# Expert stage of a delta-rule and routing kernel: 31 tiles of 128 tokens in place of 19 tiles of 256

## The chip, the cores and the metric

The kernel runs on one core of one Trainium2 chip. The metric is device time in microseconds (us), the median of several executions. One execution was also recorded by the hardware profiler, instruction by instruction. The engines are named as in its rows: PE (TensorE matmuls), PEld (TensorE weight loads, which overlap PE), DVE (VectorE), ACT (ScalarE), POOL (GpSimd) and SP (SyncE, which here only issues transfers). A "q" behind a name, as in SPq, is that engine's sequencer.

## The reference

Four sequences of 768 tokens, 8 heads of 48, go through a delta rule, and each of the 3072 output rows of 384 then goes through one of 8 experts. Everything is float32.

```
for t in range(S):                       # per batch and head
    y[t]  = q[t] @ state
    state = state + beta[t] * outer(k_n[t], v[t] - k_n[t] @ state)
x = y as [3072, 384]
expert_idx = argmax(cosine(x, expert_emb) / tau);  gate = softmax(...)[expert_idx]
for e in range(8):                       # w1[e]: 384 x 1024, w2[e]: 1024 x 384
    mask = expert_idx == e
    out[mask] = gate[mask] * (relu(x[mask] @ w1[e]) @ w2[e])
```

## The kernel before

The delta rule is worked in chunks of 128 tokens, six chunks of each sequence; a chunk inverts a 128 x 128 triangular matrix per head in six levels (`invert`: transposes on L240, products on L248 and L257, all 128 x 128). The chunk's rows and their gates are stored to `x_dram`, and each token's number is scattered into `idmap`, a list per expert in DRAM (L362, four scatters a chunk, on POOL's queue).

When all tokens are routed, a few short VectorE operations (L400 to L421) work out, for each of the tiles that the experts then run, which expert it has and where its part of the list begins. The number of tiles is fixed in the program: N / T + E - 1 with N = 3072 and E = 8, which is 19 for T = 256. It is enough for any split of the tokens; tiles that the split does not need run all the same, on list entries that name a row of zeros, and their output rows are dropped.

For a tile, `fetch(i)` reads expert and place into registers of SP and issues on SP's queue, in this order, the tile's list `ids`, the expert's `w1` (384 x 1024, 1536 KB) and its `w2` (1024 x 384, 1536 KB). POOL gathers the tile's rows `xg` from `x_dram` by those `ids`, 128 rows to an instruction. `experts` transposes the rows on PE (L447), copies them to `xTm` on DVE (L448), multiplies `w1` into `psH` (L454, moving operand 256 columns wide), applies Relu on ACT (L456), multiplies by `w2` for each half of 128 tokens (L460, moving operand 384 wide), scales by the gate on DVE (L463) and scatters the rows to `out` from POOL (L464). The pool `wt` holds the weights in two buffers, so a load of `w1` waits until PE is done with the `w1` of two tiles before.

A float32 matmul stands as two instructions in the trace (24 matmuls of L454 in a tile are 48 records), a transpose as one. The order on each engine comes from the framework's scheduler, which lets it differ a little from the order in the code.

Of the kernel before, what the change touches and what calls it, by code (L numbers as in the profile page):

```python
# [8 lines left out]
F32 = mybir.dt.float32  # L9
I32 = mybir.dt.int32  # L10
AX = mybir.AxisListType
ALU = mybir.AluOpType
ACT = mybir.ActivationFunctionType
SP = mybir.EngineType.SP

C = 128  # tokens in a chunk of the delta rule
T = 256  # tokens in a tile of the experts
LEVELS = (2, 4, 8, 16, 32, 64)
# [3 lines left out]
def kernel(  # L22
# [11 lines left out]
):  # L34
    """Delta rule in chunks of 128 tokens, then each token through its one expert, all in float32.

    In a chunk, with kb = beta k and the state S before it, z solves (I + A) z = v - k S, with
    A[t, s] = k_t . kb_s below the diagonal; then y = q S + strict_lower(q kb^T) z and S += kb^T z.
    (I + A)^-1 is put together from its diagonal blocks, of 2, 4, ... 128 rows: from the inverses of
    blocks of s rows to those of 2s rows, W = W - W A_s^T W, where W is the transposed inverse and  # L40
    A_s the part of A below the diagonal blocks of s inside those of 2s.

    A token's rank within its expert gives its place in a list of that expert's tokens (in DRAM).
    The experts then work through tiles of 256 tokens of one expert each; 256-token tiles that any
    split of the tokens needs are at most N / 256 + E - 1, and those it doesn't need are empty.
    """
    nc = tc.nc
    B, H, S, D = q.shape
    NC, NP, Dm, N = S // C, H // 2, H * D, B * S
    E, _, F = moe_w1.shape  # L50
    KC, NF = Dm // 128, F // 128
    NT = N // T + E - 1
# [4 lines left out]
    x_dram = tc.dram_tile([N + 1, Dm + 1], F32, name="x_dram")  # L57
    idmap = tc.dram_tile([NMAP, 1], I32, name="idmap")

    def big(shape):  # L60
        return ps.tile(shape, F32, name="big", tag="big", bufs=5)

    def seq(shape):
        return ps.tile(shape, F32, name="seq", tag="seq", bufs=3)

# [1 line left out]
    ident = cpool.tile([128, 128], F32, name="ident")  # L67
    make_identity(nc, ident)
    ones = cpool.tile([128, 128], F32, name="ones")
# [17 lines left out]

    # Tokens' lists name the row of zeros behind the tokens wherever no token is put in.
    none = cpool.tile([128, NMAP // 128], I32, name="none")
# [13 lines left out]

    # With x = row ^ column, x in [s, 2s) picks the blocks of s rows beside the diagonal ones.
    xor_i = ac.tile([128, 128], I32, name="xor_i")
# [23 lines left out]

# [1 line left out]
    Qp = []  # L131
    for i in range(2):
        t = ac.tile([128, B, H, 64], F32, name=f"Qp{i}")
# [3 lines left out]
    for i in range(6):  # L137
        t = ac.tile([128, 2, H, 64], F32, name=f"KK{i}")
# [27 lines left out]

    # Expert embeddings over their norms, transposed.
    esq = ac.tile([E, Dm], F32, name="esq")
# [11 lines left out]

# [1 line left out]
    def prep(c, K4):  # L182
        """k over its norm, and that times beta, padded to 64 columns a head."""
        Ksq = wk.tile([128, B, H, D], F32, name="Ksq", tag="Ksq", bufs=1)
        nc.gpsimd.tensor_tensor(Ksq, K4, K4, op=ALU.mult)
        rn = wk.tile([128, B, H], F32, name="rn", tag="rn")
        nc.vector.tensor_reduce(rn, Ksq, axis=AX.X, op=ALU.add)
        nc.gpsimd.tensor_tensor(out=rn, in0=rn, in1=half, op=ALU.pow)
        nc.vector.tensor_scalar_add(rn, rn, 1e-6)
        nc.vector.reciprocal(rn, rn)  # L190
        kks = []
        for b in range(B):
            kk = KK[(c * B + b) % len(KK)]
            nc.gpsimd.tensor_tensor(kk[:, 0, :, 0:D], K4[:, b],
                                    rn[:, b].unsqueeze(2).broadcast_to([128, H, D]), op=ALU.mult)
            nc.gpsimd.tensor_tensor(kk[:, 1, :, 0:D], kk[:, 0, :, 0:D],  # L196
                                    betaT[:, c, b].unsqueeze(2).broadcast_to([128, H, D]), op=ALU.mult)
            kks.append(kk)
        return kks

    def front(c, b, kk):
        """Transposes of k, q and kb, and the two masked products over kb."""
        KT = wk.tile([128, NP, 3, 128], F32, name="KT", tag="KT", bufs=3)
# [29 lines left out]
    def invert(groups):  # L233
        """groups: [A^T by head, W], W the transposed inverses of the diagonal blocks of 2 rows."""
        for s in LEVELS:
# [17 lines left out]
            for g, Pm in zip(groups, Ps):  # L253
                W = g[1]
# [8 lines left out]
    def back(c, b, kk, KT, LM, Ws, V, xc, ssx, lz):  # L263
        """The chunk's outputs and the next state; the logits and the norms of the outputs."""
        if c > 0:
# [39 lines left out]
        psX = big([128, KC, 128])  # L305
# [9 lines left out]
    def route(c, xc, ssx, lz):  # L315
        """Each token's expert, gate and place in its expert's list, for a chunk of each sequence."""
        def t(name, shape):
# [9 lines left out]
        nc.vector.tensor_reduce(m, lz, axis=AX.X, op=ALU.max)  # L327
        # The first of the largest.
        oh = t("oh", be)
# [56 lines left out]

# [1 line left out]
    wt = ctx.enter_context(tc.tile_pool(name="wt", bufs=2))  # L388
    mk = ctx.enter_context(tc.tile_pool(name="mk", bufs=2))
# [32 lines left out]

# [1 line left out]
    def fetch(i):  # L424
        e = nc.values_load(info[0:1, 0, i:i + 1], engines=(SP,), min_val=0, max_val=E - 1)
        s = nc.values_load(info[0:1, 1, i:i + 1], engines=(SP,), min_val=0, max_val=NMAP - T)
        ids = mk.tile([128, 2], I32, name="ids", tag="ids", bufs=4)
        nc.sync.dma_start(ids, idmap[bass.ds(s, T), :].rearrange("(p t) o -> p (t o)", t=2))
        w1 = wt.tile([128, KC, F], F32, name="w1", tag="w1")
        nc.sync.dma_start(w1, moe_w1[bass.ds(e, 1)].rearrange("o (c p) f -> p (o c) f", p=128))  # L430
        w2 = wt.tile([128, NF, Dm], F32, name="w2", tag="w2")
        nc.sync.dma_start(w2, moe_w2[bass.ds(e, 1)].rearrange("o (f p) m -> p (o f) m", p=128))
        xg = []
        for t in range(2):
            x = mk.tile([128, Dm + 1], F32, name="xg", tag="xg", bufs=6)
            nc.gpsimd.indirect_dma_start(  # L436
                out=x, out_offset=None, in_=x_dram[:, :],
                in_offset=bass.IndirectOffsetOnAxis(ap=ids[:, t:t + 1], axis=0))
            xg.append(x)
        return ids, w1, w2, xg  # L440

    def experts(ids, w1, w2, xg):
        xT = mk.tile([128, KC, T], F32, name="xTm", tag="xTm")
        for t in range(2):
            psX = big([128, KC, 128])
            for j in range(KC):
                nc.tensor.transpose(psX[:, j, :], xg[t][:, j * 128:(j + 1) * 128], ident)  # L447
            nc.vector.tensor_copy(xT[:, :, t * 128:(t + 1) * 128], psX)  # L448
        hT = mk.tile([128, NF, T], F32, name="hT", tag="hT")
        for f in range(0, NF, 2):  # L450
            psH = big([128, 2, T])
            for i in range(2):
                for j in range(KC):
                    nc.tensor.matmul(psH[:, i, :], lhsT=w1[:, j, (f + i) * 128:(f + i + 1) * 128], rhs=xT[:, j, :],  # L454
                                     start=(j == 0), stop=(j == KC - 1))
            nc.scalar.activation(hT[:, f:f + 2, :], psH, ACT.Relu)  # L456
        for t in range(2):
            psO = seq([128, Dm])
            for f in range(NF):
                nc.tensor.matmul(psO, lhsT=hT[:, f, t * 128:(t + 1) * 128], rhs=w2[:, f, :],  # L460
                                 start=(f == 0), stop=(f == NF - 1))
            y = mk.tile([128, Dm], F32, name="y", tag="y", bufs=4)
            nc.vector.tensor_scalar_mul(y, psO, xg[t][:, Dm:Dm + 1])  # L463
            nc.gpsimd.indirect_dma_start(  # L464
                out=out[:, :], out_offset=bass.IndirectOffsetOnAxis(ap=ids[:, t:t + 1], axis=0),
                in_=y, in_offset=None, bounds_check=N - 1, oob_is_err=False)

    ahead = fetch(0)
    for i in range(NT):
        now = ahead  # L470
        if i + 1 < NT:
            ahead = fetch(i + 1)
        experts(*now)

# [29 lines left out]
```

## Time and profile before

| | |
|---|---|
| time, three executions | 1692.67, 1698.79, 1700.02 us |
| median | 1698.79 us |
| span of the profiled execution, first to last instruction | 1703.2 us |
| PE busy over the span | 1476.8 us (87%) |
| mean granted clock of TensorE | 0.864 |
| first L454 matmul starts, last L463 starts | 1262.20 us, 1692.24 us |

No other time was recorded for the profiled execution than its span, which lies 4.4 us above the median. Busy times are sums over records, and a record's own duration overlaps its neighbours' where an engine is pipelined, as PE is: the pace of matmuls is read from when one line's records start to when the next line's start. [...]

### The profile page before, as it was taken

The page shows a single profiled execution, that of the slowest core. Times are in us where ns is not written, and L with a number is a line of the kernel's source. Part 1 is how long each engine was busy: PE and PEld are TensorE (multiplying, and loading weights), DVE is VectorE, ACT ScalarE, POOL GpSimd, SP SyncE. Part 2 cuts the span into 40 slices and gives each one's busy share as a digit, 9 for nine tenths or more (in the row PEclk, how much of TensorE's full clock was granted, in tenths as well). Part 3 has the DMA queues.
Part 4 walks back from the last instruction along what each step waited for, and adds up shares of the span by engine and source line. Part 5 has one row for each costly group of instructions (what it writes and reads, how often), then busy time and mean ns, then how long its engine had stood idle before and what let it go on. Part 6 is the DMA issues. An engine that isn't in the chain of part 4 may idle for free. (4 is left out here: it accounts for less than half of the span.)

```text
span 1703.2 us, 23067 instructions
## 1 busy us (share of the span) xinstructions
PE 1476.8 (87%) x9723; PEld 1318.2 (77%) x9723; DVE 568.2 (33%) x1015; ACT 318.2 (19%) x613; POOL 350.3 (21%) x330
## 2 busy tenths in 40 slices
PE   3698969989698997989889897989739999999997
PEld 2697959979597996979789796979737666677774
DVE  4542525344362543526343352625401111001010
ACT  2122222121222212122212212222100000111110
POOL 7703042020503004030310204020021111111110
PEclk9786959789697977969788896979769999999999
DMA  9100030001200010000100000000045554555540
GB/s 144 19 1 10 1 65 1 6 5 20 47 1 10 1 43 6 1 10 1 38 1 1 1 1 19 2 1 1 19 171 184 173 180 159 163 179 178 165 145 0
DMA packets 114233, 92.62 MB, mean 54 GB/s; under 512 B 81137, under 2 KB 103849, under 8 KB 114130
## 3 DMA queue, kind: packets, MB, share of 16 engines
q1 hardware_dynamic: 108290, 78.80, 16.3%
q0 software_dynamic: 5632, 12.24, 2.6%
q8 instruction: 76, 1.25, 0.3%
q14 instruction: 27, 0.22, 0.0%
q10 hardware_dynamic: 208, 0.11, 0.0%
HBM read 81.55 MB, written 12.33 MB: 55 GB/s over the span
## 5 line engine op out<-in xcount | busy, mean ns | idle before, releaser
L251 DVE TENSOR_TENSOR Pm<-big,nmask 128x512 f32<-128x512 f32 x288 | 198.1, 691 | 308.8 <-PE big L248 308.8
L248 PE MATMUL big<-Ti,LM 128*128 128x128 f32 x2304 | 290.7, 288 | 0.0
L248 PEld LDWEIGHTS big<-Ti,LM 128*128 128x128 f32 x2304 | 285.9, 206 | 0.0
L257 PE MATMUL big<-W,Pm 128*128 128x128 f32 x2304 | 271.0, 276 | 9.1 <-DVE Pm L251 9.1
L257 PEld LDWEIGHTS big<-W,Pm 128*128 128x128 f32 x2304 | 264.8, 193 | 9.5 <-DVE Pm L251 9.5
L242 ACT ACTIVATE Ti<-big 128x512 f32<-128x512 f32 x288 | 152.7, 601 | 563.9 <-PE big L240 563.9
L240 PE MATMUL big<-ident,W 128*128 128x128 f32 x1152 | 157.8, 288 | 105.3 <-POOL W L229 105.3
L240 PEld LDWEIGHTS big<-ident,W 128*128 128x128 f32 x1152 | 134.8, 148 | 120.0 <-POOL W L229 116.7
L454 PE MATMUL big<-xTm,w 128*128 128x256 f32 x912 | 204.4, 384 | 18.4 <-DVE xTm L448 18.4
L260 DVE TENSOR_TENSOR W<-big,W 128x512 f32<-128x512 f32 x288 | 199.0, 691 | 57.6 <-PE big L257 57.5
L454 PEld LDWEIGHTS big<-xTm,w 128*128 128x128 f32 x912 | 173.5, 192 | 46.3 <-DVE xTm L448 23.0
L460 PE MATMUL seq<-w,hT 128*128 128x384 f32 x608 | 199.2, 486 | 0.0
L460 PEld LDWEIGHTS seq<-w,hT 128*128 128x128 f32 x608 | 115.5, 190 | 76.5
L463 DVE TENSOR_SCALAR y<-seq,xg 128x384 f32<-128x384 f32 x38 | 23.5, 618 | 390.5 <-PE seq L460 390.5
L196 POOL TENSOR_TENSOR KK<-KK,betaT 128x384 f32<-128x384 f32 x24 | 19.8, 830 | 600.4 <-PE seq L299 600.4
L456 ACT ACTIVATE hT<-big 128x512 f32<-128x512 f32 x76 | 45.4, 597 | 407.5 <-PE big L454 407.5
L464 POOL DMA_INDIRECT out_dram<-y,ids x38 | 38.3, 1008 | 239.5 <-DVE y L463 239.5
L215 PE MATMUL big<-KT 48*128 48x256 f32 x384 | 75.1, 511 | 10.0 <-ACT KT L208 10.0
L215 PEld LDWEIGHTS big<-KT 48*128 48x128 f32 x384 | 53.1, 248 | 22.0 <-ACT KT L208 14.8
L287 PE MATMUL seq<-Z,LM 128*128 128x48 f32 x384 | 66.4, 343 | 2.3 <-ACT Z L279 2.3
L287 PEld LDWEIGHTS seq<-Z,LM 128*128 128x128 f32 x384 | 65.2, 264 | 2.9 <-ACT Z L279 2.9
L436 POOL DMA_INDIRECT xg<-x_dram,ids x38 | 37.1, 977 | 130.6 <-DMA ids<-idmap 119.7
(131 smaller groups left out, 1076.9 us busy)
## 6 DMA issues: line engine op xcount, KB each, us to landing
w<-in_moe_w_dram SPq DMA_DIRECT2D x38, 1536.0 KB, 7.0
x_dram<-xc SPq DMA_DIRECT2D x6, 770.0 KB, 4.3
K<-in_k_dram SPq DMA_DIRECT2D x24, 192.0 KB, 4.1
V<-in_v_dram SPq DMA_DIRECT2D x24, 192.0 KB, 4.1
Qp<-in_q_dram SPq DMA_DIRECT2D x24, 192.0 KB, 2.9
xg<-x_dram,ids POOLq DMA_INDIRECT x38, 3.4
out_dram<-y,ids POOLq DMA_INDIRECT x38, 3.1
idmap<-tokid,slot_i POOLq DMA_INDIRECT x24, 4.1
```

Source lines behind the costliest of these rows:

```text
L215: nc.tensor.matmul(psG[:, i], lhsT=KT[pr, 2 * g + i, 2, :], rhs=KT[pr, 2 * g + i, 0:2, :], start=True, stop=True, skip_group_check=True)
L240: nc.tensor.transpose(psI[:, j, :], W[:, j, :], ident)
L242: nc.scalar.activation(Ti, psI, ACT.Copy)
L248: nc.tensor.matmul(psP[:, j, :], lhsT=AT[:, j, :], rhs=Ti[:, j, :], start=True, stop=True, skip_group_check=True)
L251: nc.vector.tensor_tensor(Pm, psP, nmask[s].broadcast_to([128, NP, 128]), op=ALU.mult)
L257: nc.tensor.matmul(psW[:, j, :], lhsT=Pm[:, j, :], rhs=W[:, j, :], start=True, stop=True, skip_group_check=True)
L260: nc.vector.tensor_tensor(Wn, psW, W, op=ALU.add)
L287: nc.tensor.matmul(psY[:, h, :], lhsT=LM[:, h % 2, h // 2, 1, :], rhs=Z[:, h, :], start=(c == 0 and h == 0), stop=True, skip_group_check=True)
L454: nc.tensor.matmul(psH[:, i, :], lhsT=w1[:, j, (f + i) * 128:(f + i + 1) * 128], rhs=xT[:, j, :], start=(j == 0), stop=(j == KC - 1))
L456: nc.scalar.activation(hT[:, f:f + 2, :], psH, ACT.Relu)
L460: nc.tensor.matmul(psO, lhsT=hT[:, f, t * 128:(t + 1) * 128], rhs=w2[:, f, :], start=(f == 0), stop=(f == NF - 1))
L464: nc.gpsimd.indirect_dma_start(out=out[:, :], out_offset=bass.IndirectOffsetOnAxis(ap=ids[:, t:t + 1], axis=0), in_=y, in_offset=None, bou ...
```

## The change

A tile has 128 tokens, and 31 tiles are run (3072 / 128 + 7). A tile has one gather, one group of three transposes, one product with `w2` and one scatter. The product with `w1` has a moving operand 128 columns wide; four of the eight blocks of 128 hidden units share one PSUM tile and one Relu. The pool `wt` has three buffers, two fetches are issued ahead of the loop, and the transposes of the next tile are placed in front of the products of the current one. Comments that were taken out are left out here.

```diff
-T = 256  # tokens in a tile of the experts
+T = 128
...
-    wt = ctx.enter_context(tc.tile_pool(name="wt", bufs=2))
+    wt = ctx.enter_context(tc.tile_pool(name="wt", bufs=3))
...
-        ids = mk.tile([128, 2], I32, name="ids", tag="ids", bufs=4)
-        nc.sync.dma_start(ids, idmap[bass.ds(s, T), :].rearrange("(p t) o -> p (t o)", t=2))
+        ids = mk.tile([128, 1], I32, name="ids", tag="ids", bufs=5)
+        nc.sync.dma_start(ids, idmap[bass.ds(s, T), :])
...
+        x = mk.tile([128, Dm + 1], F32, name="xg", tag="xg", bufs=5)
+        nc.gpsimd.indirect_dma_start(
+            out=x, out_offset=None, in_=x_dram[:, :],
+            in_offset=bass.IndirectOffsetOnAxis(ap=ids[:, 0:1], axis=0))
+        return ids, w1, w2, x
+
+    def transposed(x):
+        xT = mk.tile([128, KC, T], F32, name="xTm", tag="xTm", bufs=3)
+        psX = big([128, KC, 128])
+        for j in range(KC):
+            nc.tensor.transpose(psX[:, j, :], x[:, j * 128:(j + 1) * 128], ident)
+        nc.vector.tensor_copy(xT, psX)
+        return xT
...
-        for f in range(0, NF, 2):
-            psH = big([128, 2, T])
-            for i in range(2):
+        for f in range(0, NF, 4):
+            psH = big([128, 4, T])
+            for i in range(4):
...
-    ahead = fetch(0)
+    ahead = [fetch(0), fetch(1)]
+    xT = transposed(ahead[0][-1])
     for i in range(NT):
-        now = ahead
-        if i + 1 < NT:
-            ahead = fetch(i + 1)
-        experts(*now)
+        now = ahead.pop(0)
+        if i + 2 < NT:
+            ahead.append(fetch(i + 2))
+        nxT = transposed(ahead[0][-1]) if ahead else None
+        experts(xT, *now)
+        xT = nxT
```

The order of PE's instructions where the experts begin, before the change. Numbers behind names are buffers: `xg_9066` and `xg_9068` are the two halves of tile 0, `xg_9096` is a half of tile 1, and `w1_9062` and `w2_9064` are the weights of tile 0; x3 counts matmuls in a row.

```order
L447 MATMUL big_9101<-ident_65,xg_9066 128x128 x3
L447 MATMUL big_9106<-ident_65,xg_9068 128x128 x3
L454 MATMUL big_9112<-xTm_9100,w1_9062 128x256 x6
...
L460 MATMUL seq_9144<-w2_9064,hT_9111 128x384 x8
L460 MATMUL seq_9158<-w2_9064,hT_9111 128x384 x8
L447 MATMUL big_9203<-ident_65,xg_9096 128x128 x3
```

The same place after the change, where `xg_9066`, `xg_9094` and `xg_9128` are tiles 0, 1 and 2.

```order
L443 MATMUL big_9097<-ident_65,xg_9066 128x128 x3
L443 MATMUL big_9131<-ident_65,xg_9094 128x128 x3
L453 MATMUL big_9137<-xTm_9096,w1_9062 128x128 x12
L453 MATMUL big_9151<-xTm_9096,w1_9062 128x128 x12
L458 MATMUL seq_9165<-w2_9064,hT_9136 128x384 x8
L443 MATMUL big_9208<-ident_65,xg_9128 128x128 x3
L453 MATMUL big_9214<-xTm_9130,w1_9090 128x128 x12
```

The transposes of tile 1 now stand in front of the products of tile 0, and those of tile 2 in front of the products of tile 1; before, a tile's transposes stood directly in front of its own products.

POOL's instructions from the first gather of the experts on, before the change; `ids_9060`, `ids_9090`, `ids_9192` and `ids_9294` are the lists of tiles 0 to 3.

```order
L436 DMA xg_9198<-x_dram_63,ids_9192 128x385
L436 DMA xg_9200<-x_dram_63,ids_9192 128x385
L464 DMA out_0_dram<-y_9153,ids_9060 3072x384
L464 DMA out_0_dram<-y_9167,ids_9060 3072x384
L436 DMA xg_9300<-x_dram_63,ids_9294 128x385
```

After the change, with `ids_9060`, `ids_9088`, `ids_9122`, `ids_9199` and `ids_9276` the lists of tiles 0 to 4.

```order
L434 DMA xg_9066<-x_dram_63,ids_9060 128x385
L434 DMA xg_9094<-x_dram_63,ids_9088 128x385
L434 DMA xg_9128<-x_dram_63,ids_9122 128x385
L461 DMA out_0_dram<-y_9174,ids_9060 3072x384
L434 DMA xg_9205<-x_dram_63,ids_9199 128x385
L461 DMA out_0_dram<-y_9251,ids_9088 3072x384
L434 DMA xg_9282<-x_dram_63,ids_9276 128x385
```

The gather of tile 3 stands behind the scatter of tile 0 in both, and the gather of tile k behind the scatter of tile k - 3 from there to tile 17; from tile 18 on the scheduler puts it behind the scatter of tile k - 4.

## Rows read from the trace of the kernel before

**Rows 1.** Page, part 2: 40 equal slices of the span, in tenths.

```profile
PE   3698969989698997989889897989739999999997
PEclk9786959789697977969788896979769999999999
DMA  9100030001200010000100000000045554555540
```

**Rows 2.** Groups by line and form, 1225 to 1700 us; busy, mean of one, idle before.

```profile
L454 PE MATMUL big<-xTm,w 128*128 128x256 f32 x912 | 204.4, 384 | 18.4 <-DVE xTm L448 18.4
L454 PEld LDWEIGHTS big<-xTm,w 128*128 128x128 f32 x912 | 173.5, 192 | 46.3 <-DVE xTm L448 23.0
```

**Rows 3.** Timeline of one tile: start, us, engine, line, what, count, idle before.

```profile
1353.23 0.82 PE L447 MATMUL big<-ident,xg 128*128 128x128 f32 x6
1353.44 0.62 DVE L463 TENSOR_SCALAR y<-seq,xg 128x384 f32<-128x384 f32 x1 [4.54 <-PE seq L460]
1354.34 1.00 POOL L464 DMA_INDIRECT out_dram<-y,ids  x1 [4.14 <-DVE y L463]
1355.04 10.22 PEld L454 LDWEIGHTS big<-xTm,w 128*128 128x128 f32 x48 [1.22 <-DVE xTm L448]
1355.04 10.63 PE L454 MATMUL big<-xTm,w 128*128 128x256 f32 x48 [0.98 <-DVE xTm L448]
1365.50 10.48 PE L460 MATMUL seq<-w,hT 128*128 128x384 f32 x32
1375.82 0.82 PE L447 MATMUL big<-ident,xg 128*128 128x128 f32 x6
```

**Rows 4.** Waits of SP's own queue, 1240 to 1703 us: total, times, longest.

```profile
SPq L430 <- PE big L454: 177.7, 17, 11.0
SPq L432 <- PE big L447: 165.8, 17, 10.0
```

**Rows 5.** Timeline in the last chunk's inversion, PE alone.

```profile
1173.39 3.74 PE L248 MATMUL big<-Ti,LM 128*128 128x128 f32 x32
1176.96 3.74 PE L257 MATMUL big<-W,Pm 128*128 128x128 f32 x32
1180.54 1.91 PE L240 MATMUL big<-ident,W 128*128 128x128 f32 x16
1182.28 3.74 PE L248 MATMUL big<-Ti,LM 128*128 128x128 f32 x32
```

**Rows 6.** Windows: us, busy (records) of PE, PEld, DVE, ACT, POOL; PEclk, DMA share, GB/s.

```profile
1173.39:1180.54 7.15, 7.15 (x67) 7.15 (x66) 4.84 (x7) 1.01 (x3) 0.00 (x0) 1.00 0.01 2
...
1353.04:1375.62 22.58, 21.60 (x88) 15.83 (x87) 2.17 (x4) 2.39 (x4) 3.98 (x4) 1.00 0.53 170
1260.00:1265.00 5.00, 4.29 (x13) 2.96 (x12) 1.11 (x2) 0.00 (x0) 0.95 (x1) 0.50 1.06 385
```

**Rows 7.** Timeline where the experts begin.

```profile
1252.62 2.34 SPq L428 DMA_DIRECT2D ids<-idmap  x1
1253.69 0.98 POOL L436 DMA_INDIRECT xg<-x_dram,ids  x1 [5.09 <-issue]
1259.71 1.83 PE L447 MATMUL big<-ident,xg 128*128 128x128 f32 x6 [28.58 <-DMA xg<-x_dram,ids]
1262.19 12.72 PEld L454 LDWEIGHTS big<-xTm,w 128*128 128x128 f32 x48 [1.05 <-DVE xTm L448]
1262.20 13.12 PE L454 MATMUL big<-xTm,w 128*128 128x256 f32 x48 [0.65 <-DVE xTm L448]
1264.03 0.95 POOL L436 DMA_INDIRECT xg<-x_dram,ids  x1 [8.10 <-DMA ids<-idmap]
```

**Rows 8.** Tile xg: gathers' time to landing, 1263 to 1275 us, then 1250 to 1703.

```profile
DMA to landing us min/median/max: 3.6/6.4/6.5
...
DMA to landing us min/median/max: 3.0/3.4/7.0
```

**Rows 9.** Page, part 6: issues, KB each, median us from issue to landing.

```profile
w<-in_moe_w_dram SPq DMA_DIRECT2D x38, 1536.0 KB, 7.0
```

**Rows 10.** Timeline at the end of the span.

```profile
1692.24 0.62 DVE L463 TENSOR_SCALAR y<-seq,xg 128x384 f32<-128x384 f32 x1 [4.54 <-PE seq L460]
1693.13 0.98 POOL L464 DMA_INDIRECT out_dram<-y,ids  x1 [4.17 <-DVE y L463]
```

More of the change, by code (lines that the diff above doesn't have):

```diff
@@ L432, in fetch, with experts @@
         nc.sync.dma_start(w2, moe_w2[bass.ds(e, 1)].rearrange("o (f p) m -> p (o f) m", p=128))
[L433 to L448, printed above, removed]
+        x = mk.tile([128, Dm + 1], F32, name="xg", tag="xg", bufs=5)
[10 more added lines that the diff above has]
+        return xT
+    def experts(xT, ids, w1, w2, x):
         hT = mk.tile([128, NF, T], F32, name="hT", tag="hT")
-        for f in range(0, NF, 2):
-            psH = big([128, 2, T])
-            for i in range(2):
+        for f in range(0, NF, 4):
+            psH = big([128, 4, T])
+            for i in range(4):
                 for j in range(KC):
@@ L455, in experts @@
                                      start=(j == 0), stop=(j == KC - 1))
[L456 to L466, printed above, removed]
-    ahead = fetch(0)
-    for i in range(NT):
-        now = ahead
-        if i + 1 < NT:
-            ahead = fetch(i + 1)
-        experts(*now)
+            nc.scalar.activation(hT[:, f:f + 4, :], psH, ACT.Relu)
+        psO = seq([128, Dm])
+        for f in range(NF):
+            nc.tensor.matmul(psO, lhsT=hT[:, f, :], rhs=w2[:, f, :], start=(f == 0), stop=(f == NF - 1))
+        y = mk.tile([128, Dm], F32, name="y", tag="y", bufs=4)
+        nc.vector.tensor_scalar_mul(y, psO, x[:, Dm:Dm + 1])
+        nc.gpsimd.indirect_dma_start(
+            out=out[:, :], out_offset=bass.IndirectOffsetOnAxis(ap=ids[:, 0:1], axis=0),
+            in_=y, in_offset=None, bounds_check=N - 1, oob_is_err=False)
+    ahead = [fetch(0), fetch(1)]
+    xT = transposed(ahead[0][-1])
+    for i in range(NT):
+        now = ahead.pop(0)
[4 more added lines that the diff above has]
+        xT = nxT
 _INS = ['q', 'k', 'v', 'beta', 'moe_expert_emb', 'moe_tau', 'moe_w1', 'moe_w2']
```

## The prediction

> **What bounds the kernel now.** I read the 40 slices first: one slice is 42.6 us, and from the 30th on PE is busy in nine tenths at a granted clock near full speed while the DMA engines are about half busy; before that stands the delta rule, which the change does not touch [rows 1]. So the change is worth what it does to the last 440 us. Next come the groups of that stretch, to see what PE waits for there: 18.4 us, all for the copy `xTm`, about 1 us at each of 19 tiles [rows 2]. The timeline of one tile shows the period. From one start of the transposes to the next are 1375.82 - 1353.23 = 22.59 us: 1.81 us until L454 starts (six transposes, then the wait for the copy), 10.46 us until L460 starts, and 10.32 us until the next transposes [rows 3]. SP's own waits say the same from the other side: both weight loads wait for PE to release a buffer, 177.7 and 165.8 us in total, so loads are late for nobody [rows 4]. The stage is bound by PE's matmuls, at full clock, with DMA at 0.53 [rows 6].
>
> **The change, part by part.**
>
> *w1 products.* A tile has as many of them as before, 48 records, but 128 columns wide. The expert stage has no such row; the inversion has one of the same shape and type, 128 columns against a 128 x 128 float32 weight: 64 of them go from 1173.39 to 1180.54, 7.15 us, 0.1117 us each [rows 5], at clock 1.00 [rows 6]. So 48 cost 5.36 us, against 10.46 / 48 = 0.218 us each at 256 columns. Bounds: half of the latter (0.109) from below; from above 0.192, the duration of one weight load of L454 [rows 2], if loads no longer hid behind the shorter matmuls. I take 0.1117 because that row's weight load has the same size. Going from w1 to w2 adds 0.2 us, as now: the 48 loads take 10.22 us, and L460 starts 10.46 us after L454 [rows 3].
>
> [...]
>
> *w2 products.* 16 records of the same width in place of 32: 16 x 10.32 / 32 = 5.16 us [rows 3].
>
> *Transposes.* Three a tile, at the pace of L240, 16 in 1.74 us [rows 5]: 0.33 us. The copy that followed them, and PE's wait for it, leave the path, since they now have a whole tile of products as cover. If that cover failed, the 0.98 us of wait [rows 3] would come back at each tile, 30 us in all.
>
> *One tile* is then 5.36 + 0.2 + 5.16 + 0.33 = 11.05 us. Relu handles the same 512 columns at a time as now, and the second Relu of a tile is covered by the first 8 records of w2 (2.6 us).
>
> *31 tiles.* From the first L453 to the end of the last L458: 31 x 10.72 = 332.3 us, 29 groups of transposes in between 9.6 us, and the start at half clock. That cost 12.72 - 10.22 = 2.5 us in the first tile before [rows 3, 7]; I take 3.5, since PE now sits idle between the first transposes and the rest. Sum 345.4 us. Before, the same stretch went from 1262.20 to 1692.24 [rows 7, 10], 430.0 us. Gain 84.6 us.
>
> *The first tile starts later.* PE works in order, and the transposes of tile 1 stand before the products of tile 0. Tile 1's list is issued at 1252.62 behind 3 MB of weights, and its gather can start only at 1264.03, when the list has landed [rows 7]. Gathers of that moment, beside streaming weights, took 3.6 to 6.5 us to land, median 6.4 [rows 8], so x is there at 1270.4; with the semaphore and three transposes at half clock (0.9 us; six and a wait took 1.83 [rows 7]) L453 starts at about 1271.4 instead of 1262.20. Loss 9.2 us, between 6.4 and 9.8.
>
> *Loads.* A tile moves 3.15 MB of weights, 0.20 MB of gather and 0.20 MB of scatter, 3.54 MB. At the 385 GB/s seen where transfers stood in line [rows 6] that is 9.2 us, 83% of 11.05. At the price that transfers had in the old tile, 0.53 x 22.58 us for 170 GB/s x 22.58 us = 3.84 MB [rows 6], it is 11.0 us. I take the first, since transfers will stand in line again. With three buffers a `w1` is issued when PE leaves that of three tiles before, almost two tiles before its use (20 us), and takes 7.0 us to land when alone [rows 9]: cost nothing. If the cover were gone, DMA's 11.0 us would be the period, which is the same.
>
> *Gathers.* On POOL's queue the gather of tile k stands behind the scatter of tile k - 3. That scatter ends 2.11 us after PE leaves its tile (1353.23 to 1355.34 [rows 3]); the gather lands 3.4 to 7.0 us after its issue [rows 8]. So x is there 5.8 to 9.4 us after that point and needed 11.05 us after it. Cost nothing, with 1.7 us to spare in the worst case.
>
> *The end* is unchanged: DVE, one scatter, and what follows, 1703.2 - 1692.24 = 11.0 us [rows 10]. The tables of 31 entries are made beside four scatters into `idmap`; nothing.
>
> *Sum:* -84.6 + 9.2 = -75.4 us on a span of 1703.2 us, which lies 4.4 us above the median of 1698.79 us: 1627.8 us as a span, **1623 us** as a median.
>
> **Rivals.**
>
> *Gathers come late.* DMA is 83 to 100% busy, so landing may take longer than the 7.0 us seen. Beyond 8.7 us each microsecond stalls PE at tiles 3 to 17 (later tiles are issued a tile earlier). At 10 us: 1.3 x 15 = 20 us, and about 36 us if it holds at all tiles: 1643 to 1659. For it speaks the thin margin; against it that a gather beside fully streaming weights landed in 6.5 us [rows 8].
>
> *The shorter matmul does not hide its weight load.* At 0.192 us a product [rows 2] the tile is 14.9 us, and 31 x 3.86 = 120 us are lost against the forecast: 1743, slower than before. It decides from about 13.5 us a tile on, where (430.0 - 9.2 - 3.5) / 31 eats the gain, that is from 0.163 us a product. Against it stands the 0.1117 of the inversion [rows 5]. [...]
>
> *Weights do not stream.* If each load began only when the one before had landed, two of 7.0 us [rows 9] make the tile 14.0 us: 31 x 2.95 = 91 us, 1714, slower. Against it: SP waited for PE and not for a landing [rows 4], and loads in line moved 385 GB/s [rows 6].
>
> *The transposes are not ahead in effect.* If PE still waited for each copy: +30 us, 1653. The order after the change speaks against it, since a tile's products stand behind a copy made a tile earlier.
>
> **How the numbers follow.** The forecast has 82%: 1610 to 1638, from 0.109 us a product (-4 us), the two bounds of the head (-3, +1), the half clock (-1 to +3), and up to 0.3 us a tile of changeover that no row shows (+9). Late gathers or waiting transposes have 9%, weight loads exposed in part 3% (1691, within 0.5% of before), in full 3% (1743), loads one by one 3% (1714). So I say 1623 us with a range of 1608 to 1655. A difference of under 0.5% (8.5 us) is about what a measurement of this kernel cannot tell from none, since its three runs spread over 0.43%. Faster by more than that 0.92, within it 0.03, slower 0.05.
>
> **What would show it.** In the changed trace, L453 starts should follow each other every 11.05 us; 48 of its records should take 5.4 us; L453 should show no wait for `xTm`, and L443 none for `xg` beyond tiles 0 and 1; PE should sit idle for some 9 us between tile 0's transposes and tile 1's; the DMA share should be 0.83 to 1.0. The forecast is wrong if L453's records take over 0.13 us each, if L443 waits for `xg` in the steady state, or if L453 or L458 wait for `w`.

## The result, and the profile after

The changed kernel takes 1605.57 us (median of four, 1603.40 to 1610.42) against 1695.73 us before in the same comparison; the ratio is 0.9475, 95% interval 0.9435 to 0.9515. It is faster, as forecast, but the median lies 2.4 us under the range. Two later comparisons of the same kernel gave 0.9501 (0.9457 to 0.9546) and 0.9509 (0.9483 to 0.9535), so 5% is the better figure. One execution of this kernel (6286 us) and one of the kernel before (7816 us) in the later comparisons are left out of every figure here.

The profiled execution spans 1604.3 us. These are the slices that answer to [rows 1]; a slice is now 40.1 us.

```profile
PE   3698997989879898798988989799892799999997
PEclk9796978979779797897968999598895799999999
DMA  9100021000210002000010000000001999999991
```

From the 33rd slice to the 39th PE is as full as before, and now so are the DMA engines, at nine tenths in place of four or five. One tile in the timeline, to hold against [rows 3]:

```profile
1410.16 0.49 PE L443 MATMUL big<-ident,xg 128*128 128x128 f32 x3
1410.37 0.62 DVE L460 TENSOR_SCALAR y<-seq,xg 128x384 f32<-128x384 f32 x1 [9.77 <-PE seq L458]
1410.49 5.52 PE L453 MATMUL big<-xTm,w 128*128 128x128 f32 x48
1411.26 1.02 POOL L461 DMA_INDIRECT out_dram<-y,ids  x1 [8.56 <-DVE y L460]
1412.58 0.97 POOL L434 DMA_INDIRECT xg<-x_dram,ids  x1 [0.30 <-issue]
1415.85 5.33 PE L458 MATMUL seq<-w,hT 128*128 128x384 f32 x16
1421.01 0.49 PE L443 MATMUL big<-ident,xg 128*128 128x128 f32 x3
```

From L443 to L443 are 10.85 us: 0.33 for the transposes, 5.36 for w1, 5.16 for w2, and no wait. 5.36 / 48 is 0.1117 us a record, what the inversion had shown [rows 5]. The groups of 1225 to 1605 us, which answer to [rows 2], show that the wait for `xTm` is gone:

```profile
L453 PE MATMUL big<-xTm,w 128*128 128x128 f32 x1488 | 173.1, 277 | 0.0
L453 PEld LDWEIGHTS big<-xTm,w 128*128 128x128 f32 x1488 | 170.7, 194 | 0.3
```

The windows of one tile and of most of the stage, as in [rows 6]: us, busy of PE, PEld, DVE, ACT and POOL, granted clock, DMA share, GB/s.

```profile
1323.36:1334.21 10.85, 10.85 (x68) 8.68 (x67) 1.08 (x2) 1.19 (x2) 1.99 (x2) 1.00 0.94 324
...
1280.00:1550.00 270.00, 270.00 (x1673) 216.36 (x1672) 27.04 (x50) 29.87 (x50) 49.65 (x50) 1.00 0.96 323
```

PE has no gap in 270 us, at full clock. The place where the experts begin, as in [rows 7]:

```profile
1237.48 0.37 SPq L428 DMA_DIRECT2D ids<-idmap  x1
...
1247.26 0.87 PE L443 MATMUL big<-ident,xg 128*128 128x128 f32 x3 [29.27 <-DMA xg<-x_dram,ids]
...
1249.77 0.95 POOL L434 DMA_INDIRECT xg<-x_dram,ids  x1 [8.14 <-DMA ids<-idmap]
...
1256.01 0.90 PE L443 MATMUL big<-ident,xg 128*128 128x128 f32 x3 [7.88 <-DMA xg<-x_dram,ids]
...
1256.71 7.41 PE L453 MATMUL big<-xTm,w 128*128 128x128 f32 x48
...
1269.44 5.52 PE L453 MATMUL big<-xTm,w 128*128 128x128 f32 x48
```

PE does tile 0's transposes, sits idle for 7.88 us until tile 1's rows have landed, and only then starts on w1, 19.2 us after the first list's issue; before it was 1262.20 - 1250.92 = 11.3 us.

**Where the time went.** From the issue of the first list to the end of the span were 1703.2 - 1250.9 = 452.3 us before and are 1604.3 - 1237.5 = 366.8 us now: 85.5 us gained, 5.03% of 1698.79. The other 13.4 us between the two spans lie in the delta rule, whose first list came at 1250.9 us in one execution and at 1237.5 us in the other.

### The profile page after: what moved, and what is told of

Read it like the earlier page. It is cut to its first block, busy times and chain, and to the rows that moved or that the text cites. A ratio compares the mean times of both kernels' runs of the same rounds, so it can differ in the third digit from the quotient of the medians.

```text
span 1604.3 us, 24107 instructions
## 1 busy us (share of the span) xinstructions
PE 1389.4 (87%) x10166; PEld 1275.2 (79%) x10166; DVE 561.2 (35%) x1001; ACT 309.6 (19%) x599; POOL 336.1 (21%) x316
## 3 DMA queue, kind: packets, MB, share of 16 engines
q0 software_dynamic: 4736, 10.85, 1.9%
## 5 line engine op out<-in xcount | busy, mean ns | idle before, releaser
L453 PE MATMUL big<-xTm,w 128*128 128x128 f32 x1488 | 173.1, 277 | 0.0
L458 PE MATMUL seq<-w,hT 128*128 128x384 f32 x496 | 165.1, 486 | 0.0
L458 PEld LDWEIGHTS seq<-w,hT 128*128 128x128 f32 x496 | 91.9, 190 | 57.5
L460 DVE TENSOR_SCALAR y<-seq,xg 128x384 f32<-128x384 f32 x31 | 19.1, 618 | 305.0 <-PE seq L458 305.0
L455 ACT ACTIVATE hT<-big 128x512 f32<-128x512 f32 x62 | 37.0, 598 | 336.4 <-PE big L453 291.3
L215 PE MATMUL big<-KT 48*128 48x256 f32 x384 | 71.1, 487 | 10.1 <-ACT KT L208 10.1
L461 POOL DMA_INDIRECT out_dram<-y,ids x31 | 31.5, 1018 | 163.2 <-DVE y L460 159.8
L228 POOL TENSOR_TENSOR W<-LM,nmask 128x512 f32<-128x512 f32 x48 | 60.7, 1265 | 10.2 <-DVE LM L220 9.2
```

The source lines that it names most:

```text
L215: nc.tensor.matmul(psG[:, i], lhsT=KT[pr, 2 * g + i, 2, :], rhs=KT[pr, 2 * g + i, 0:2, :], start=True, stop=True, skip_group_check=True)
L228: nc.gpsimd.tensor_tensor(W, LM[:, hh, :, 0, :], nmask1.broadcast_to([128, NP, 128]), op=ALU.mult)
L455: nc.scalar.activation(hT[:, f:f + 4, :], psH, ACT.Relu)
L458: nc.tensor.matmul(psO, lhsT=hT[:, f, :], rhs=w2[:, f, :], start=(f == 0), stop=(f == NF - 1))
```

## The experiments

Below, "to the end" means the span less the time at which the first list was issued. It leaves the delta rule out. A period is the time from one tile's start to the next tile's, at the same line. Edits are shown against the changed kernel unless said otherwise, and lines that they only take away are left out.

### Is the delta rule faster, or is it one execution against another?

The kernels before and after, unchanged.

> The kernel before, unchanged, profiled once more. In the first pair of profiles the first list of the experts was issued at 1250.92 us before and at 1237.48 us after the change, 13.4 us earlier, in a stage that the change was thought not to touch. Theory (the delta rule's length is a matter of how long TensorE stands at half clock in one execution: 441 us before, 404 us after): this profile gives some other time for that issue, anywhere from 1235 to 1255 us, in step with its half-clock time, and the ratio to itself is 1.00. Rival (the change shortened the delta rule): 1251 us again within 2 us.

> The changed kernel, unchanged, profiled once more and timed in five rounds. Theory (expert stage alone): from the issue of the first list to the end 357.0 + 9.8 = 367 us again within 1 us, and a ratio of 0.950 (85 us of 1696). Rival (the delta rule gained too): ratio 0.943 to 0.945, and the first list again near 1237 us.

Measured: before against itself 1.000 (0.9975 to 1.0026), first list at 1245.46 us, to the end 451.9 us. After: ratio 0.9501 (0.9457 to 0.9546), first list at 1233.48 us, to the end 367.1 us. The expert stage repeats within 0.4 us in these pairs; the delta rule does not, 5.5 us between two executions of one program. A third profile of the changed kernel, run beside the later experiments:

> The changed kernel once more, for a comparison on the same chip as the three runs beside it and a further profile of the delta rule. From the first list to the end 367 us, ratio 0.950.

Measured: 0.9509 (0.9483 to 0.9535), first list at 1238.52 us, to the end 367.6 us. All three give 84 to 85.5 us for the stage, and the two ratios are what the stage alone gives (0.950). In the third profile one tile was late, with a period of 12.09 us: a gather landed after 9.5 us, and PE stood for it.

```profile
1337.16 0.97 POOL L434 DMA_INDIRECT xg<-x_dram,ids  x1 [0.30 <-issue]
...
1346.80 0.52 PE L443 MATMUL big<-ident,xg 128*128 128x128 f32 x3 [1.05 <-DMA xg<-x_dram,ids]
```

Five executions put the first list at 1250.9 and 1245.5 before and 1237.5, 1233.5 and 1238.5 after, which by itself looks like a gain. But the run of the early transposes at 256 tokens (below) has the instructions of the delta rule in the very order of the kernel before, on every engine, and issued its first list at 1239.47. The eight variants with tiles of 128 tokens have them in the order of the changed kernel, and stood anywhere from 1232.1 to 1247.9. The granted clock over the stretch up to the first list goes with it only in part: 0.82 in both profiles of before, 0.83 or 0.84 in the others, 0.83 at 1247.9 as at 1233.5. The window from the start to the first list (columns as above), first of the kernel before in its second profile:

```profile
0.00:1245.46 1245.46, 1065.26 (x8089) 1015.84 (x8089) 526.65 (x939) 272.96 (x537) 275.05 (x254) 0.82 0.09 16
```

The same window of the changed kernel in its first profile:

```profile
0.00:1237.48 1237.48, 1050.10 (x8089) 1003.72 (x8089) 527.44 (x939) 272.54 (x537) 274.58 (x254) 0.84 0.09 16
```

The same 8089 records of PE are in both. The rival, that the change shortened the delta rule, finds no support in the two ratios, and its forecast for the second profile of before (1251 us again) failed; with two profiles of before it isn't excluded for a few microseconds.

### The parts by themselves

The size alone: two weight buffers, one fetch ahead, transposes in front of their own products.

```diff
-    wt = ctx.enter_context(tc.tile_pool(name="wt", bufs=3))
+    wt = ctx.enter_context(tc.tile_pool(name="wt", bufs=2))
...
+    ahead = fetch(0)
     for i in range(NT):
+        now = ahead
+        if i + 1 < NT:
+            ahead = fetch(i + 1)
+        experts(transposed(now[-1]), *now)
```

> Tiles of 128 tokens alone: two weight buffers, one fetch ahead, a tile's transposes right in front of its own products. Theory: PE waits for the copy of the transposes in each tile, about 1.1 us in a period of 12.0 us in place of 10.85 (31 x 1.15 = 36 us lost against the full change), and the first tile starts 8 us earlier since it doesn't wait for tile 1's rows: about 1605 + 28 = 1633 us, ratio 0.963. Rival (two buffers are too few at this rate of loads): PE also waits for weights, period above 12.5 us, over 1650 us.

Measured: 1633.45 us, 0.963 (0.9588 to 0.9671), all periods 11.96 us, to the end 392.7 us. Each tile shows the wait that the early transposes take away:

```profile
1419.63 0.49 PE L443 MATMUL big<-ident,xg 128*128 128x128 f32 x3
1420.37 0.55 DVE L444 COPY xTm<-big 128x384 f32<-128x384 f32 x1
1420.97 5.62 PE L453 MATMUL big<-xTm,w 128*128 128x128 f32 x48 [0.85 <-DVE xTm L444]
```

1.34 us from the transposes to w1, against 0.33. Now the other parts without the size: 256 tokens, three buffers, two fetches ahead, transposes ahead. This edit is against the kernel before.

```diff
-    wt = ctx.enter_context(tc.tile_pool(name="wt", bufs=2))
+    wt = ctx.enter_context(tc.tile_pool(name="wt", bufs=3))
...
+    def transposed(xg):
+        xT = mk.tile([128, KC, T], F32, name="xTm", tag="xTm", bufs=3)
...
+        return xT
+
+    def experts(xT, ids, w1, w2, xg):
...
+    ahead = [fetch(0), fetch(1)]
+    xT = transposed(ahead[0][-1])
     for i in range(NT):
+        now = ahead.pop(0)
+        if i + 2 < NT:
+            ahead.append(fetch(i + 2))
+        nxT = transposed(ahead[0][-1]) if ahead else None
+        experts(xT, *now)
+        xT = nxT
```

> Tiles of 256 tokens as before, but with the other parts of the change: three weight buffers, two fetches ahead, transposes one tile ahead. Theory: only the wait for the copy goes, 22.59 - 1.15 = 21.4 us a tile, 19 x 1.15 = 22 us gained, 8 to 9 us lost at the first tile: 13 us gained, ratio 0.992. The smaller tile then carries the rest, about 70 us. Rival (the parts gain only together, the third buffer and the early transposes being what the stage lacked): ratio below 0.98.

Measured: 1678.64 us, 0.9899 (0.9866 to 0.9933), a period of 1431.75 - 1410.41 = 21.34 us in place of 22.59, to the end 437.5 us.

```profile
1410.41 0.82 PE L447 MATMUL big<-ident,xg 128*128 128x128 f32 x6
...
1431.75 0.82 PE L447 MATMUL big<-ident,xg 128*128 128x128 f32 x6
```

So the size gives 62 us by itself and the rest 17 us; the rival that the parts gain only together falls. On top of the smaller tile the rest is worth more, 392.7 - 367.1 = 25.6 us of the stage, since the wait for the copy then falls away 31 times and not 19. Last, three buffers and two fetches with the transposes late (the loop of the change, with `experts(transposed(now[-1]), *now)`):

> The change without its early transposes: 128 tokens, three weight buffers, two fetches ahead, a tile's transposes right in front of its own products. Theory: the wait for the copy, 1.1 us a tile, is all that the early transposes take away, and the third buffer gives nothing, so this is the run of the size alone once more: period 11.96 us, ratio 0.963. Rival (third buffer and second fetch help by themselves): ratio 0.955 or below.

Measured: 0.9615 (0.9582 to 0.9648), periods 11.96 us, to the end 392.6 us, the size alone within 0.1 us. Third buffer and second fetch give nothing without the early transposes.

### What the third buffer is for

```diff
-    wt = ctx.enter_context(tc.tile_pool(name="wt", bufs=3))
+    wt = ctx.enter_context(tc.tile_pool(name="wt", bufs=2))
```

> The change with two weight buffers instead of three. Theory: with two, a load of w1 is issued 5.4 us into the tile two before its use, 16 us ahead, and lands in 9.5 us; PE waits for nothing, period 10.85 us, ratio 0.950 as the full change. Rival (with the DMA engines 96% busy the third buffer is what keeps PE fed): PE waits for weights, period above 11.2 us, ratio above 0.956.

Measured: 1684.98 us, 0.9932 (0.9909 to 0.9955), mean period 13.47 us, to the end 446.0 us. My theory fell: two buffers cost 79 us of the stage. But PE never waits for weights in that trace, only for gathered rows. This is its one wait from 1240 us on (total, times, longest), and a stretch of the timeline:

```profile
PE big L443 <- DMA xg<-x_dram,ids: 93.5, 22, 28.7
...
1407.46 0.37 SPq L428 DMA_DIRECT2D ids<-idmap  x1
...
1416.28 0.97 POOL L434 DMA_INDIRECT xg<-x_dram,ids  x1 [7.52 <-DMA ids<-idmap]
...
1423.66 0.88 PE L443 MATMUL big<-ident,xg 128*128 128x128 f32 x3 [6.00 <-DMA xg<-x_dram,ids]
...
1424.33 7.97 PE L453 MATMUL big<-xTm,w 128*128 128x128 f32 x48
```

The list goes out at 1407.46, right behind a load of `w2` that waited for PE. The gather that needs it starts 8.8 us later; in the start of the changed kernel, where no weights were issued ahead of the first list, that took 1240.65 - 1237.48 = 3.2 us. PE can go on 7.4 us after the gather's start, and has stood for 6 us. Then w1 takes 7.97 us; in the tile before it took 5.52 (at 1406.97), as it does at a granted clock of 1.00 in the changed kernel. After the wait the granted clock is 0.50:

```profile
1423.66:1427.00 3.34, 3.34 (x16) 3.34 (x17) 0.56 (x1) 0.00 (x0) 0.00 (x0) 0.50 0.71 265
```

So the third buffer releases the weight load, and with it the list behind it, one tile earlier. To test that, lists and gathers were taken out of `fetch` into `rows` and issued three tiles ahead, and the loads, now `weights`, two ahead as in the change:

```diff
...
+    got = [rows(0), rows(1), rows(2)]
+    ws = [weights(got[0][0]), weights(got[1][0])]
+    xT = transposed(got[0][2])
     for i in range(NT):
+        if i + 3 < NT:
+            got.append(rows(i + 3))
         if i + 2 < NT:
+            ws.append(weights(got[i + 2][0]))
+        nxT = transposed(got[i + 1][2]) if i + 1 < NT else None
...
```

> The same with two weight buffers. The full change with two buffers lost 74 us, and its trace shows PE waiting for gathered rows and not for weights. Theory (with two buffers the next list stands on SP's queue behind a load that waits for PE one tile longer, and list, gather and transposes then follow each other within a tile): with the lists issued a tile earlier two buffers are enough, periods 10.85 us, ratio 0.945 to 0.947. Rival (two buffers starve PE of weights): ratio above 0.96 and waits of PE for w.

Measured, this with two weight buffers: 0.946 (0.9427 to 0.9493), to the end 360.7 us, the two longest periods (from w2 to w2) 11.66 and 10.91 us and all others 10.85 or less. Two buffers are enough for the weights; what the third one bought was the list's place in the queue.

### The start, and POOL's order

The lists of tiles 0 to 2 ahead of the first weights, the rest as changed:

```diff
...
+    first = [lists(0), lists(1), lists(2)]
+    ahead = [fetch(0, first[0]), fetch(1, first[1])]
...
+            ahead.append(fetch(i + 2, first[2] if i == 0 else None))
```

> The change with the lists of tiles 0 to 2 issued on SP's queue ahead of the first weights. Theory (tile 1's rows are late because its list stands behind 3 MB of weights): the two gathers follow each other, PE starts w1 of tile 0 some 11 us after the first list's issue instead of 19 to 20, 7 to 8 us gained against the full change, ratio 0.945. Rival (rows are late because gathers are slow beside streaming weights): the start moves by less than 3 us, ratio 0.950.

Measured: 0.949 (0.9461 to 0.9519), to the end 369.6 us, no better than the change. Yet the start moved as the theory says: w1 begins 1259.87 - 1247.92 = 11.95 us after the first list.

```profile
1247.92 1.39 SPq L428 DMA_DIRECT2D ids<-idmap  x3
...
1259.87 7.55 PE L457 MATMUL big<-xTm,w 128*128 128x128 f32 x48
```

It was given back at one place, where a period is 20.76 us from w2 to w2. POOL's order there, from the gather of tile 2 on:

```order
L438 DMA xg_9128<-x_dram_63,ids_9104 128x385
L465 DMA out_0_dram<-y_9174,ids_9060 3072x384
L465 DMA out_0_dram<-y_9251,ids_9082 3072x384
L438 DMA xg_9205<-x_dram_63,ids_9199 128x385
```

The scheduler has put the gather of tile 3 behind the scatter of tile 1, where the change has it in front. The trace at that place:

```profile
1284.37 1.00 POOL L465 DMA_INDIRECT out_dram<-y,ids  x1 [9.83 <-DVE y L464]
1285.68 0.98 POOL L438 DMA_INDIRECT xg<-x_dram,ids  x1 [0.30 <-issue]
...
1291.78 0.87 PE L447 MATMUL big<-ident,xg 128*128 128x128 f32 x3 [8.35 <-DMA xg<-x_dram,ids]
...
1292.45 6.58 PE L457 MATMUL big<-xTm,w 128*128 128x128 f32 x48
```

The scatter waits for tile 1's last product, the gather waits for the scatter, and PE for the gather: 8.35 us, and another microsecond at half clock (granted 0.50 from 1291.78 to 1294.00; w1 takes 6.58 us in place of 5.52). The run with rows three ahead has the lists first too, and the gather of tile 3 in front of that scatter:

> The change with lists and gathers taken apart from the weights and issued three tiles ahead: the lists of tiles 0 to 2 stand in front of all weights, and on POOL's queue the gather of tile 3 stands in front of the scatter of tile 1, where the run with the lists first had it behind. Theory (tile 1's rows cost the full change 8 us at the start, and POOL's order cost the run with the lists first 9.9 us at tile 2): the first product starts 12 us after the first list's issue, all periods are 10.85 us, from the first list to the end 359 us in place of 367, ratio 0.945. Rival (the stall at tile 2 comes from the crowd of weights at the start and not from POOL's order): one period near 20 us again, ratio 0.950.

Measured: 0.9444 (0.9407 to 0.9482), median 1602.75 us against 1609.02 us of the changed kernel beside it; first product 1256.75 - 1244.69 = 12.06 us after the first list, every period from w2 to w2 10.85 us but the last (10.52, without transposes), to the end 359.7 us against 367. PE waits for rows once, before the first tile:

```profile
PE big L446 <- DMA xg<-x_dram,ids: 30.8, 1, 30.8
```

The theory holds, and this version beats both kernels; the two ratios' intervals only just part, but the 7 us stand in the profile as well.

### How near are the DMA engines to setting the pace?

One more load of `w2` per tile, into a tile that nobody reads:

```diff
+        w3 = wt.tile([128, NF, Dm], F32, name="w3", tag="w3", bufs=2)
+        nc.sync.dma_start(w3, moe_w2[bass.ds(e, 1)].rearrange("o (f p) m -> p (o f) m", p=128))
```

> The change with one more load of w2 in each tile, into a tile that nobody reads: 5.11 MB a tile in place of 3.54. It tells how near the DMA engines are to setting the pace: their busy share is 0.96 of a period already, but at 323 GB/s. Theory (the share counts packets that wait; in line they move 385 GB/s): period 13.3 us, 31 x 2.4 = 76 us more than the full change, about 1682 us, ratio 0.993. Rival (0.96 is the whole truth, 323 to 340 GB/s is the limit beside running matmuls): period 15.0 to 15.8 us, 1735 to 1760 us, ratio above 1.02.

Measured: 1768.59 us, 1.0413 (1.0365 to 1.0461). It looks like the rival's number and is not: between the first and the last, periods from w2 to w2 alternate between 10.85 and 21.0 to 22.5 us. The scheduler had put two scatters in front of two gathers, and PE waited some 8 us for rows at every other tile. The run is inconclusive on DMA, and was made again with rows three ahead:

> Rows three ahead, and the third load per tile that nobody reads. The first run with a third load alternated between periods of 10.85 and 21 to 22 us because POOL's order had two scatters in front of two gathers, so it told nothing about the DMA engines. Here the order is as in the change. Theory (in line, packets move at 385 GB/s): 5.11 MB in 13.3 us, ratio 0.99. Rival (0.96 busy at 323 GB/s was the limit): 15.0 to 15.8 us, ratio above 1.02.

Measured: 0.9879 (0.9841 to 0.9918), mean period 13.25 us, to the end 430.2 us. Its window (columns as above):

```profile
1300.00:1600.00 300.00, 256.98 (x1499) 200.87 (x1497) 26.47 (x45) 26.87 (x45) 44.66 (x46) 0.97 1.05 384
```

5.11 MB at 384 GB/s are 13.3 us, the period, and PE now waits for rows at almost every tile, some 2 us. So a busy share of 0.96 at 323 GB/s in the changed kernel left a sixth of the rate unused.

## Why the prediction was off

*The bound, the mechanism and the sign* were right: PE's products set the pace, before and after, and "what would show it" came out but for the sizes: a period of 10.85 us in place of 11.05, and an idle PE of 7.88 us at the start in place of 9. One sign did not hold in every profile: see *Gathers*.

*w1 products* were right to the fourth digit, 0.1117 us. The step that failed is the next one: "Going from w1 to w2 adds 0.2 us, as now". It adds nothing: the lines start 5.36 and 5.16 us apart, and nothing is between. I had read it from 48 loads that end 0.24 us before L460 starts, but the last of them ends 0.41 us ahead of the last product (1365.26 and 1365.67 [rows 3]), and the 0.1117 us already counted from one line's start to the next line's. 31 x 0.2 = 6.2 us of the sum were not there; the tile is 10.85 us and not 11.05. The range let that term only grow (+9 us), not vanish. No run shows the pace behind the 1691 us of weight loads exposed in part: w1 took 0.1117 us a record, and PE had no gap in 270 us.

*w2 products and transposes*: 5.16 and 0.33 us, as predicted.

*The start at half clock*: 3.5 us predicted; the first tile took 1269.44 - 1256.71 = 12.73 us, 1.9 more than the others (1.1 and 1.2 more in the other two profiles of this kernel); the granted clock was 0.50 from 1256.00 to 1260.00.

*The first tile starts later*: 9.2 us predicted, 7.95 measured, and its cause is shown: with the lists first it is 0.7 us. The list behind 3 MB on its own queue let tile 1's gather start 9.1 us after tile 0's (1240.65 to 1249.77); with the lists first it starts 1.3 us after it (1251.09 to 1252.37). A gather, from POOL's queue, landed in 5.7 to 8.1 us beside streaming weights.

*The end*: from the last DVE instruction to the end 1604.3 - 1594.48 = 9.8 us, not the 11.0 of before.

```profile
1594.48 0.62 DVE L460 TENSOR_SCALAR y<-seq,xg 128x384 f32<-128x384 f32 x1 [9.90 <-PE seq L458]
```

It goes with the size of the tile: 9.8 us in all eleven profiles with 128 tokens, 10.9 in all three with 256, the run with the early transposes among them. Why was not tried.

Together 6.2 + 1.6 + 1.25 + 1.1 = 10.2 us: the sum of -75.4 should have been some -85.5. Taken from the median at hand, 1698.79, that is 1613 us, inside the range. Of the remaining 8 us to 1605.57, 3 are before's median, which was 1695.73 with one more run. Another 2.5 are the four executions at hand: over the fifteen of the three comparisons the changed kernel's median is 1608.09, and seven of them lie under 1608. Whether the median fell inside the range was thus chance; the last 2 us are less than the fifteen spread (1602.17 to 1618.58), and their cause stays open. The range had no term for the delta rule, whose length moved by up to 19 us from one profile to the next; that was its second fault.

*Gathers*: "1.7 us to spare in the worst case" was optimistic, and nearly wrong. Beside loads that fill DMA to 0.96, gathers of the steady state landed in 5.7 to 8.1 us, median 7.2, where I had 3.4 to 7.0; the prediction's limit was 8.7, and the trace's is 1421.01 - 1412.58 = 8.4 us from a gather's issue to the transposes that need it.

```profile
DMA to landing us min/median/max: 5.7/7.2/8.1
```

The slowest had 0.3 us to spare in that profile. In the third profile of the same kernel the slowest took 9.5 us, and PE waited 1.05 us at that tile, as shown above. In the second one the slowest took 8.7 us, and one period was 10.94.

The rival of late gathers, given 9% together with that of the waiting transposes, is what stood behind the losses of three variants: two buffers, the lists first, the third load. Its price there was not the overdue microseconds alone: after a wait of 6.0, 8.35 and 8.3 us, w1 took 7.97, 6.58 and 6.86 us in place of 5.52.

*Loads*: right that PE never waits for weights, wrong in why three buffers matter; the prediction costed the third buffer by the weights' cover and did not follow the list behind them.

## What to carry to other kernels

When a tile shrinks, price its matmuls from a row of the same width and type elsewhere in the trace, from line start to line start, and add nothing for the changeover, which was nothing here (0.33, 5.36 and 5.16 us are the 10.85 of the period). Give the range a term for the stage that the change does not touch, if its length differs between executions. Then follow the small transfers, not the large ones: here a list queued behind a weight load inherited that load's wait (its gather started 8.8 us after it, with two buffers), and a gather queued behind a scatter inherited the scatter's wait for the last product (PE stood 8.35 us, with the lists first). Read the order on the issuing queues of every variant before trusting what it says, since moving three lists, or adding one load, turned it here.

## What was not expected of the hardware

SP itself was held up while it issued: in the changed kernel's start L428 took 5.57 and 5.66 us to issue a list of 0.5 KB, with four and six loads of 1536 KB issued before it, where its median is 0.35 us.

```profile
1243.97 5.57 SPq L428 DMA_DIRECT2D ids<-idmap  x1
```

After PE waits of 6.0, 8.3 and 8.35 us (two buffers, third load, lists first) the three transposes took 0.88, 0.88 and 0.87 us in place of 0.49, and the w1 products that followed 7.97, 6.86 and 6.58 us in place of 5.52; the granted clock after the first and the last of these waits was 0.50. The DMA engines moved 384 GB/s over 300 us while PE ran matmuls in 86% of them, as much as in the 5 us of [rows 6].
